# Two local reorderings in a fused attention and feed-forward kernel: the products of the last two row blocks, and one transpose moved from the sync queue to TensorE

**The chip, the cores and the metric.** The kernel runs on one core of one Trainium2 chip. The metric is the device time of one execution in microseconds; the profiled span (first to last instruction) is some 1.8 us shorter than that time in most executions. A run is called fast unless it is over 1.5% above the fastest of its kernel; only fast runs are compared.

## The reference, cut to what matters

Attention with random features for 8 batches of 576 rows, followed by a gated feed-forward layer over all 4608 rows:

```python
q_p, k_p = (phi(q_s), phi(k_s))            # phi: project on omega, exp of (h - max)
kv  = np.einsum('bhsm,bhsd->bhmd', k_p, v)
z   = np.sum(k_p, axis=2)
num = np.einsum('bhsm,bhmd->bhsd', q_p, kv)
den = np.einsum('bhsm,bhm->bhs', q_p, z)[..., None] + 1e-06
x   = (num / den)                           # -> (4608, 512)
g, val = x @ w_gate, x @ w_val
out = (gelu(g) * val) @ w_out
```

## The kernel before

The order of work on each engine is written out by hand, so an engine runs its instructions in program order. The rows are worked off in nine token tiles of 512, while a batch has 576 rows, so a block of 128 x rows can straddle two tiles. A block is normalised by VectorE (`nx`), then transposed into `xT`, either by the sync queue (`xd`) or by TensorE into PSUM and a copy (`xt`, `xc`):

```python
def xd(self, i):
    n, x_sb = self.xs[i]
    put_x(self.b * S + 2 * i * SP, n, lambda dst, o, m: nc.sync.dma_start_transpose(
        out=dst, in_=x_sb[o:o + m, :]))     # put_x: one call for each tile that is touched

def xt(self, i):
    n, x_sb = self.xs[i]
    self.xps[i] = mo_tile([P, N_DM, P], BF16, "xt_ps")      # one of four banks
    for c in range(N_DM):
        nc.tensor.transpose(self.xps[i][:, c, :n], x_sb[:n, c * P:(c + 1) * P], ident[:n, :n])

def xc(self, i, copy):
    put_x(self.b * S + 2 * i * SP, self.xs[i][0],
          lambda dst, o, m: copy(dst, self.xps[i][:, :, o:o + m]))
```

The two matrix products of a row block are done by a scheme of seven half-size products. `pm(s, n, ...)` is product n of row block s; 1, 6, 7 and 4 accumulate in the same bank, out_one, one after the other, and in between the bank is read out: `pa(s, 2)` adds product 7's sum to the right half, `pc` copies product 4's sum as the left half. `pst` stores through two queues, 64 rows each.

```python
        p.pm(0, 7, 0, HF)
        p.pa(0, 2)
        p.pm(0, 4, 0, HF)
        p.pc(0, dve)
        p.pst(0, 1, None, (nc.sync, nc.scalar))
        p.pm(1, 7, 0, HF)
        p.pa(1, 2)
        p.pst(1, 1, 1, (nc.sync, nc.scalar))      # right half
        p.pm(1, 4, 0, HF)
        p.pc(1, dve)
        p.pst(1, 1, 0, (nc.sync, nc.scalar))      # left half
```

In this text "nd group" stands for the eight small products that give one block of num and den, "gate product" for the products with w_gate (g_ps), "kz product" for the 72 that sum k_p with v, "features" for the products with omega (pq, pk) and their exponentials, and "fillers" for products of zeros that nobody reads (fill_ps). A bank is one accumulator of TensorE's output memory; four of them are handed out in turn by `mo_tile`.

The softmax here doesn't subtract the row's maximum and nothing guards it: scores larger than these inputs give would overflow.

## Time and profile before

| | before |
|---|---|
| time, median of 4 runs | 343.07 us (342.66 to 343.44) |
| TensorE busy | 327.4 of 341.0 us |
| TensorE's wait for block 3 of batch 1 | 1.03 us at 66 us |
| its two waits for VectorE in the tail | 0.52 us each |
| last copy to the end of the span | 3.3 us (337.65 to 341.0) |

(41 of TensorE's 3155 matmul records are missing from this profile.) TensorE is all but full, so a microsecond that is saved must come out of one of its waits, or of the closing part after its last product. The profile lines are in the prediction, each with what is to be seen in it.

### The profile page before, as it was taken

The numbers are of one execution on the slowest core, as the hardware profiler recorded it, in microseconds if no ns is written. First come the engines' busy times: TensorE is split into PE (matmuls) and PEld (weight loads), VectorE is DVE, ScalarE is ACT, GpSimd is POOL, SyncE is SP. The second block draws the span as 40 slices with busy tenths as digits, with TensorE's granted clock in tenths as the row PEclk, the third lists the DMA queues.
The fourth block names the chain that finished last, engine by engine and source line by source line (L and its number), as shares of the span: only waits on it lengthen the run. The fifth ranks groups of instructions, "written<-read, shape, count | busy, mean of one in ns | idle before, by whom it ended". The sixth has DMA issues, their size and how long they took to land.

```text
span 341.0 us, 7993 instructions
## 1 busy us (share of the span) xinstructions
PE 327.4 (96%) x3114; PEld 206.0 (60%) x3155; DVE 229.1 (67%) x481; ACT 214.3 (63%) x434; POOL 149.9 (44%) x152
## 2 busy tenths in 40 slices
PE   7889999889999999999999999999999999999994
PEld 3565455566646664566447654665466786686683
DVE  3875388979773768375936683677457777796783
ACT  4894366774778558756875677658765447626640
POOL 8326004033486447744674559477968400000000
PEclk9999999999999999999999999999999999999999
DMA  8999999599889256945498629671413040013004
GB/s 155 275 206 207 206 272 206 137 174 236 178 135 331 49 102 91 326 89 108 60 326 113 116 32 291 164 111 19 94 33 63 8 115 11 1 32 93 2 0 124
DMA packets 67173, 45.08 MB, mean 132 GB/s; under 512 B 47296, under 2 KB 60096, under 8 KB 67136
## 3 DMA queue, kind: packets, MB, share of 16 engines
q0 software_dynamic: 14848, 22.12, 31.4%
q1 hardware_dynamic: 51744, 21.64, 30.4%
q10 hardware_dynamic: 544, 0.82, 0.8%
q8 instruction: 24, 0.39, 0.5%
q14 instruction: 13, 0.11, 0.1%
HBM read 37.78 MB, written 9.44 MB: 138 GB/s over the span
## 4 chain that ended last, share of the span: by engine, by line
PE 83%; DVE 6%; DMA 3%; ACT 3%; issue 2%; POOL 2%; DVEq 0%; POOLq 0%
PE g_ps L433 20%; PE o_ps L559 18%; PE val_one L378 11%; PE val_two L378 9%; PE out_one L533 5%; PE out_two L533 3%; PE v_ps L462 3%; PE g_ps L425 3%; PE kz_ps L285 3%; DMA q_in<-in_q_dram 2%; PE nd L302 2%; PE pk L220 2%; DVE x_sb L314 2%; PE pq L242 2%; DVE val_c L387 1%
## 5 line engine op out<-in xcount | busy, mean ns | idle before, releaser
L433 PE MATMUL g_ps<-xT,w_gate_sb 128*128 128x512 bf16 x352 | 108.2, 379 | 0.5
L440 ACT ACTIVATE g_gelu<-g_ps 128x512 bf16<-128x512 f32 x108 | 63.6, 598 | 54.1 <-PE g_ps L433 25.3
L559 PE MATMUL o_ps<-w_out_sb,gated 128*128 128x512 bf16 x275 | 64.6, 380 | 1.1 <-issue 0.6
L480 POOL TENSOR_TENSOR gated<-g_gelu,val_c 128x512 bf16<-128x512 bf16 x29 | 33.7, 1164 | 52.2 <-DVE iden L313 26.3
L387 DVE TENSOR_TENSOR val_c<-val_one,val_c 128x256 f32<-128x256 f32 x48 | 20.3, 424 | 49.0 <-ACT g_gelu L440 40.0
L378 PEld LDWEIGHTS <-w_val_sb 128*128 128x128 bf16 x384 | 36.5, 98 | 17.3 <-issue 1.4
L559 PEld LDWEIGHTS <-gated 128*128 128x128 bf16 x288 | 26.5, 98 | 33.5 <-issue 3.9
L383 ACT COPY val_c<-val_one 128x256 f32<-128x256 f32 x95 | 35.2, 371 | 11.2 <-PE val_one L378 8.1
L378 PEld LDWEIGHTS <-val_sums 128*128 128x128 bf16 x288 | 27.3, 98 | 24.4 <-DVE x_sb L314 3.7
L249 ACT ACTIVATE q_pT<-pq 128x512 bf16<-128x512 f32 (+1 forms) x68 | 34.6, 598 | 11.7 <-PE pq L242 11.5
L233 DVE TENSOR_REDUCE nmax<-pk 128x8 f32<-128x1024 f32 (+2 forms) x43 | 39.7, 968 | 2.9 <-PE pk L220 1.4
L433 PEld LDWEIGHTS <-w_gate_sb 128*128 128x128 bf16 x376 | 34.9, 98 | 11.2
L228 ACT ACTIVATE k_p<-pk 128x1024 bf16<-128x1024 f32 (+2 forms) x43 | 33.0, 832 | 8.1 <-PE pk L220 6.4
L378 PE MATMUL val_one<-x_sums,w_val_sb 128*128 128x256 bf16 x192 | 36.6, 272 | 0.6 <-DVE val_c L387 0.4
L387 DVE TENSOR_TENSOR val_c<-val_two,val_c 128x256 f32<-128x256 f32 x96 | 36.0, 414 | 0.8 <-PE val_two L378 0.7
L271 POOL TENSOR_TENSOR v_ext<-vf,wk 128x1152 bf16<-128x1152 f32 x12 | 28.2, 2347 | 13.9 <-ACT wk L260 13.9
L484 POOL TENSOR_TENSOR gated<-g_gelu,val_c 128x256 bf16<-128x256 bf16 x34 | 24.1, 711 | 15.0 <-ACT g_gelu L440 15.0
L314 DVE TENSOR_TENSOR x_sb<-nd,iden 128x512 bf16<-128x512 f32 (+2 forms) x41 | 27.8, 677 | 1.4
L564 DVE COPY o_sb<-o_ps 128x512 f32<-128x512 f32 x20 | 13.7, 685 | 19.4 <-PE o_ps L559 14.9
L383 ACT COPY val_c<-val_two 128x256 f32<-128x256 f32 x45 | 16.8, 373 | 11.7 <-PE val_two L378 11.7
L484 DVE TENSOR_TENSOR gated<-g_gelu,val_one 128x256 bf16<-128x256 bf16 x48 | 20.0, 416 | 6.0 <-ACT g_gelu L440 5.7
L378 PE MATMUL val_two<-x_sums,val_sums 128*128 128x256 bf16 x96 | 18.4, 274 | 1.0 <-POOL x_sums L455 0.3
(104 smaller groups left out, 486.3 us busy)
## 6 DMA issues: line engine op xcount, KB each, us to landing
out_dram<-o_sb SPq DMA_DIRECT2D x67, 128.0 KB, 3.3
vf<-in_v_dram POOLq DMA_DIRECT2D x7, 1152.0 KB, 12.4
q_in<-in_q_dram POOLq DMA_DIRECT2D x8, 576.0 KB, 9.4
k_in<-in_k_dram POOLq DMA_DIRECT2D x7, 576.0 KB, 6.2
w_gate_sb<-in_moe_w_gate_dram POOLq DMA_DIRECT2D x3, 512.0 KB, 17.7
w_val_sb<-in_moe_w_val_dram POOLq DMA_DIRECT2D x3, 512.0 KB, 19.4
w_out_sb<-in_moe_w_out_dram POOLq DMA_DIRECT2D x3, 512.0 KB, 13.4
vf<-in_v_dram SPq DMA_DIRECT2D x1, 1152.0 KB, 5.7
```

What stands on the lines that cost most here:

```text
L228: last["begun"] = nc.scalar.activation(self.k_p[:, gs, i0:i0 + n, :], pk, func=Exp)
L233: nc.vector.reduce_max(self.nmax[:, gs, i0:i0 + n], pk, axis=AX, negate=True)
L249: last["begun"] = nc.scalar.activation(dst[:, a, i0:i0 + n], self.pq[c][a].rearrange("m (i e p) -> m i e p", e=2, p=SP), func=Exp)
L314: nc.vector.tensor_mul(x_sb[:n].rearrange("p (g h d) -> p g h d", g=2, h=4)[:, gs], ndv[:, :, :, :D], iden[:n, gs].broadcast_to((n, gs.sto ...
L378: nc.tensor.matmul(ps, w[:, c, self.i * P:(self.i + 1) * P], x[:, c], start=first and c == 0, stop=c == 1, skip_group_check=not first)
L383: copy(self.c[:, {1: 0, 6: 1, 5: 2}[n]], self.beta if n == 5 else self.one)
L387: nc.vector.tensor_add(part, (self.gamma, self.beta, self.one)[k], part)
L433: last["begun"] = nc.tensor.matmul(self.gps[jf], w_gate_sb[:, jm, jf * P:(jf + 1) * P], x_tiles[self.t][:, jm], start=(jm == 0), stop=(jm ...
L440: nc.scalar.activation(self.gelus[jf][:, part], src, func=Gelu)
L480: eng.tensor_mul(self.gated[:, i, :], self.gelus[i], self.v[i].row())
L484: eng.tensor_mul(self.gated[:, i + HF, ts], self.gelus[i + HF][:, ts], s.c[:, 2] if half else s.one)
L559: nc.tensor.matmul(self.ps[qq], self.g.gated[:, f, qq * P:(qq + 1) * P], w_out_sb[:, f, :], start=(jf == 0), stop=(jf == N_DFF - 1))
```

## The change

The intent is to close the two kinds of wait named in the table. In the tail both seventh products go first, so that VectorE reads one block's bank while TensorE works on the other's. Block 3 of batch 1 leaves the queue in which it stood fourth, and goes over TensorE.

```diff
         n.nx(3)
-        n.xd(3)
         m.kf(2, False)
         m.km(2)
         fill(12)
+        n.xt(3)
+        n.xc(3, dve)
         m.kf(3, True)
@@
         p.pm(0, 7, 0, HF)
         p.pa(0, 2)
+        p.pm(1, 7, 0, HF)
+        p.pa(1, 2)
         p.pm(0, 4, 0, HF)
         p.pc(0, dve)
         p.pst(0, 1, None, (nc.sync, nc.scalar))
-        p.pm(1, 7, 0, HF)
-        p.pa(1, 2)
-        p.pst(1, 1, 1, (nc.sync, nc.scalar))
         p.pm(1, 4, 0, HF)
         p.pc(1, dve)
-        p.pst(1, 1, 0, (nc.sync, nc.scalar))
+        p.pst(1, 1, None, (nc.sync, nc.scalar))
```

## The prediction

> **What bounds the kernel now.** I read the page first: its header, the busy line and the chain that ended last.
>
> ```profile
> span 341.0 us, 7993 instructions
> PE 327.4 (96%) x3114; PEld 206.0 (60%) x3155; DVE 229.1 (67%) x481; ACT 214.3 (63%) x434; POOL 149.9 (44%) x152
> ...
> PE 83%; DVE 6%; DMA 3%; ACT 3%; issue 2%; POOL 2%; DVEq 0%; POOLq 0%
> ```
>
> TensorE is busy for 327.4 of 341.0 us, so all of its idle time is 13.6 us, and 83% of the chain is its own work. A change that only reorders work can win no more than the particular holes that it closes. The two parts of this change aim at two different holes, so I then read the chain in order of time around the first one (the columns are start in us, length in us, what):
>
> ```profile
> 62.95 0.42 DVE x_sb L314
> ...
> 63.38 0.76 DVE nmax L233
> ...
> 65.05 2.33 DMA xT<-x_sb
> ...
> 67.57 1.38 POOL x_sums L455
> ```
>
> Between 65.05 and 67.38 the end of the program hangs on a transposing transfer into xT, and then on the Pool subtraction that reads it. The timeline of the same place says what TensorE does meanwhile (start, length, engine, line, operation, and in brackets the idle time before it with its releaser):
>
> ```profile
> 65.95 0.44 PE L302 MATMUL nd<-kz,q_pT 128*64 128x65 bf16 x8
> 67.42 0.61 PE L425 MATMUL g_ps<-xT,w_gate_sb 128*128 128x256 bf16 x4 [1.03 <-DMA xT<-x_sb]
> ```
>
> It stands for 1.03 us. Cutting the sync queue's own timeline into short windows gives the five transposes of batch 1 that are queued there: they are issued at 60.64, 62.43, 63.73, 65.05 and 66.34. The first three are x blocks 0 to 2; the last two are block 3, in two because its 128 rows straddle two token tiles. They land 2.8, 2.4, 2.5, 2.3 and 2.4 us after issue. Block 3 was ready on VectorE at 63.37 (62.95 + 0.42) but its turn in the queue came only at 65.05, and it landed at about 67.4. That is the wait.
>
> The second hole is the tail. The timeline there, TensorE first and then VectorE:
>
> ```profile
> 333.06 0.82 PE L533 MATMUL out_one<-w_out_sb,gated 128*128 128x256 bf16 x6
> 334.40 0.81 PE L533 MATMUL out_one<-out_sums,gated 128*128 128x256 bf16 x6 [0.52 <-DVE o_sb L544]
> 335.05 0.82 PE L533 MATMUL out_one<-w_out_sb,gated 128*128 128x256 bf16 x6
> 336.38 0.81 PE L533 MATMUL out_one<-out_sums,gated 128*128 128x256 bf16 x6 [0.52 <-DVE o_sb L544]
> ```
>
> ```profile
> 333.92 0.42 DVE L544 TENSOR_TENSOR o_sb<-out_one,o_sb 128x256 f32<-128x256 f32 x1 [0.16 <-PE out_one L533]
> 335.25 0.42 DVE L547 COPY o_sb<-out_one 128x256 f32<-128x256 f32 x1 [0.91 <-PE out_one L533]
> 335.90 0.42 DVE L544 TENSOR_TENSOR o_sb<-out_one,o_sb 128x256 f32<-128x256 f32 x1 [0.23 <-PE out_one L533]
> 337.23 0.42 DVE L547 COPY o_sb<-out_one 128x256 f32<-128x256 f32 x1 [0.91 <-PE out_one L533]
> ```
>
> Each row block's fourth product adds onto the bank that its seventh product has just filled, so TensorE waits twice, 0.52 us each, for VectorE to read the seventh one out. After the last copy (337.65) nothing is left but the last stores.
>
> **What the Trainium skill says.** "VectorE: DVE Perf Modes", section "The three transpose paths", gives 390 ns for a 128x128 bf16 transpose on TensorE and 1309 ns by DMA. The trace agrees in kind: one transpose record on TensorE has a median of 218 ns and the records overlap (four start within 0.22 us in the chain), against 2.3 to 2.8 us to landing here. "TensorE: Matmul & The Clock Gate", section "Part 4: PE-mode transpose", adds that the result goes to PSUM and has to be copied out; the trace has the price of such a copy:
>
> ```profile
> L330 PE MATMUL xt_ps<-ident,x_sb x20: 190/218/229, 21.5 to 42.3; 128*128 128x128 bf16 x16, 64*128 64x64 bf16 x4
> ...
> L335 DVE COPY xT<-xt_ps x4: 284/418/425, 22.8 to 42.9; 128x512 bf16<-128x512 bf16 x3, 128x256 bf16<-128x256 bf16 x1
> ```
>
> "DMA: Bandwidth & Descriptors", section "Issuing engines are not separate DMA queues", says that stores issued from two engines run on the same 16 DMA engines and interleave. The trace agrees: of two stores of 128 KB issued together at 333.79, behind an earlier pair, the sync one lands after 2.4 us and the scalar one only after 3.1, where the lone last pair of 64 KB takes 1.9 and 2.2. This matters for the tail.
>
> **Part two, the transpose (first in time).** Removed: two DMA transposes out of the sync queue. Added on TensorE: four transposes, 0.22 us of issue, placed after the fillers and before the next features, where TensorE already waits until about 63.44 for VectorE's block 3. Added on VectorE: two copies of 128x256 (block 3 goes to two tiles) at 0.284 us, about 0.5 us together, between two of the maxima. Their own path: block 3 ready 63.37, transposed by about 63.85; VectorE is in a maximum of 1.22 us from 63.29, so the copies run from 64.42 to about 64.95. Block 3 is thus there 2.4 us earlier than its transfer landed.
>
> What then comes last? Tile 1 also needs block 2, whose transfer is issued at 63.73 and lands at 66.2. And the standing order of TensorE puts the fifth nd group first: 65.95 before, about 0.2 later now, since the transposes push the features, these push the scalar exponentials, and these free its bank. With its 0.26 us of issue (eight at 0.03) that is 66.45. So the gate product that stood until 67.42 starts at about 66.45: **0.97 us** earlier. The Pool subtraction moves from 67.54 to about 66.35.
>
> How much survives? Step by step: the q features at 67.97 need VectorE's delayed maximum and ScalarE's last k exponentials, about 66.9; they move to about 67.1, 0.87 earlier. ScalarE's exponentials of these were at 68.39; its copy of o_ps is now delayed 0.3 to 0.4 by the later wk and ends at about 67.5, so they start there: 0.9 earlier. The next product of that bank was at 69.79 behind ScalarE's copy at 69.36, so also 0.9 earlier. VectorE, 0.5 us loaded at 65, has slack again by the subtraction at 68.97, which was waiting 1.04 us for Pool and moves by about 1.1. Both roads give about 0.9 at the kz product at 73.12. From there to 92 TensorE is busy for 18.69 of 18.88 us (table of windows), and in the later steps hardly anything but TensorE is on the chain, so the shift should arrive at the end whole: I take **0.9 us**, between 0.6 and 1.1.
>
> **Part one, the tail.** Nothing is added; two 64 KB stores of the second block's right half and two of its left half become two of 128 KB. Six matmuls take 0.655 us of issue (334.40 to 335.05), the last ends 0.82 after the first starts. New order: seventh of block 0 at 333.06; seventh of block 1 at 333.71, ends 334.53; VectorE's addition of block 0 unchanged, 333.92 to 334.34; fourth of block 0 at 334.40 as before, with the hole filled; addition of block 1 from 334.56 to 334.98; fourth of block 1 at 335.05, no wait, ends 335.87; copy of block 0 at 335.25 as before, copy of block 1 from 335.90 to 336.32. Compute thus ends 337.65 - 336.32 = 1.33 us earlier.
>
> But the end is a landing, not a copy. Before: last pair issued 337.69, landing 2.2 later, 339.9, and 1.1 us of closing to 341.0. Now 256 KB are issued at 335.70 and 256 KB at about 336.37, 0.67 apart. The same pattern is in the trace: 256 KB at 333.13 and 256 KB at 333.79, where the last one landed 3.1 us after its issue. So the end is 336.37 + 3.1 = 339.5 instead of 339.9: about 0.4 us. If the larger stores landed like a lone pair of 128 KB (2.7) it would be 0.8. I take **0.5 us**, since two thirds of what is won in compute is given back to the transfer of bytes that formerly left earlier.
>
> **Sum.** 343.06 - 0.9 - 0.5 = 341.66; I say 341.6, for the span some 339.6.
>
> **Rivals.** (a) The wait is only replaced at 66: if block 2's landing or the bank behind ScalarE gives no more than half of the hole, part two is worth 0.4 and the time 342.2. For it: both come within 0.3 us of my new start. Against: neither is above 66.5. (b) PSUM rotation: the extra bank for the transposes shifts which bank each later tile takes in the pool of four, one of which is held by an unfinished o_ps and one by the first gate tile. If the gate tile or the q features get a bank that is freed late, TensorE waits as long as before, the 0.5 us on VectorE is a loss, and the time is 342.6 to 343.2. The trace speaks against a large one, as the copies end before 64.99, when the first gate product starts anyway. (c) The gain of part two is swallowed by something timed independently, the loads of the third batch, or by VectorE, up to 92: then only the tail remains, 342.5. Against: these loads are issued behind the very Pool subtraction that moves forward. (d) The tail gives its full 1.3 us because the last stores overlap better: 340.8.
>
> **Range and chances.** My centre is the sum; (a) to (c) bound it above at 342.6, (d) with a full first part below at 340.7. Three runs of before differ by 0.42 us, which is part of the width. Two per cent is 6.9 us, far beyond both holes together (1.03 + 1.33 us), so within 2% is nearly certain; what is left is for a lost overlap that I cannot see.
>
> **What would show it.** Right: the wait of 1.03 us before the second gate product gone or below 0.2, that product at 66.3 to 66.7; three transposes instead of five in the sync queue; the kz product near 72.2; the later steps unchanged in length (35.4 us from one to the next); in the tail the 0.52 us waits gone, the last copy 1.3 us nearer to its first product, and about 2.9 to 3.1 us from last issue to landing. Wrong: a new wait of TensorE on a bank at 64 to 68, ScalarE or VectorE ahead of kz, or a shift at 73 that is gone at 92.

## The result, and the profile after

The changed kernel took 341.95 us (median of 4, 341.57 to 342.13) against 343.07 in the same rounds. A ratio in this text is the mean time of one kernel's fast runs over that of the other's of the same rounds, so it is not quite the ratio of the medians; here it is 0.9966, 95% interval 0.9949 to 0.9983. The means are 341.90 and 343.06, 1.16 us apart. The prediction's 341.6 lies 0.35 below the median, which lies inside the range.

The page of the changed kernel, the same three lines as in the prediction:

```profile
span 340.1 us, 7996 instructions
PE 328.1 (96%) x3118; PEld 206.9 (61%) x3159; DVE 229.5 (67%) x483; ACT 214.3 (63%) x434; POOL 149.5 (44%) x152
...
PE 84%; DVE 7%; issue 2%; ACT 2%; DMA 2%; POOL 1%; SPq 0%; DVEq 0%
```

TensorE has four instructions more, and the transfers' share of the chain went from 3 to 2%. The timeline of TensorE where the first wait was (start, length, engine, line, operation):

```profile
65.73 0.60 PE L425 MATMUL g_ps<-xT,w_gate_sb 128*128 128x256 bf16 x4 [0.27 <-DMA xT<-x_sb]
...
66.69 0.44 PE L302 MATMUL nd<-kz,q_pT 128*64 128x65 bf16 x8
67.06 0.61 PE L425 MATMUL g_ps<-xT,w_gate_sb 128*128 128x256 bf16 x4
```

The second gate product now follows the fifth nd group without a wait in brackets. A wait for a transfer is left at the first gate product, 0.27 us here and 0.17 before; it comes back under "Why the prediction was right". VectorE's two new copies, and the sync queue with three transposes in place of five:

```profile
64.85 0.48 DVE L335 COPY xT<-xt_ps 128x256 bf16<-128x256 bf16 x2
```

```profile
61.06 4.59 SPq L322 DMA_TRANSPOSE xT<-x_sb  x3
```

In this first profile everything up to 60 us ran about 0.4 us later than in that of before, although both kernels have the same instructions there. So positions are best measured from the first nd group of batch 1 (59.23 before, 59.65 after): the second gate product starts 8.19 us after it before and 7.41 after, the kz product 13.89 and 12.93.

The tail, TensorE and then VectorE:

```profile
332.60 1.47 PE L533 MATMUL out_one<-w_out_sb,gated 128*128 128x256 bf16 x12
...
333.94 1.47 PE L533 MATMUL out_one<-out_sums,gated 128*128 128x256 bf16 x12
```

```profile
333.46 0.42 DVE L544 TENSOR_TENSOR o_sb<-out_one,o_sb 128x256 f32<-128x256 f32 x1 [0.16 <-PE out_one L533]
334.11 0.42 DVE L544 TENSOR_TENSOR o_sb<-out_one,o_sb 128x256 f32<-128x256 f32 x1 [0.23 <-PE out_one L533]
334.79 0.42 DVE L547 COPY o_sb<-out_one 128x256 f32<-128x256 f32 x1 [0.25 <-PE out_one L533]
335.45 0.42 DVE L547 COPY o_sb<-out_one 128x256 f32<-128x256 f32 x1 [0.23 <-PE out_one L533]
```

Two runs of twelve matmuls have replaced four of six, and both 0.52 us waits are gone. The last copy ends 3.27 us after the start of the first seventh product (335.87 less 332.60) instead of 4.59: 1.32 us won. But the span ends 4.27 us after that copy instead of 3.31 (read from the trace to the nanosecond, as the span on the page is rounded): 0.96 us of it are given back. The list of transfers shows where. The scalar queue's last store before the change, then after it (engine and operation, count, size, us from issue to landing):

```profile
out_dram<-o_sb ACTq DMA_DIRECT2D x1, 64.0 KB, 2.2
```

```profile
out_dram<-o_sb ACTq DMA_DIRECT2D x1, 128.0 KB, 3.1
```

It is issued at 337.69 before and 335.90 after, so it lands at 339.9 and 339.0; the remaining 1.1 us to the end of the span are the same in both.

### The profile page after: what moved, and what is told of

Its sections match the earlier page's. It is cut to its first block, busy times and chain, and to the rows that moved or that the text cites. A ratio compares the mean times of both kernels' runs of the same rounds, so it can differ in the third digit from the quotient of the medians.

```text
span 340.1 us, 7996 instructions
## 1 busy us (share of the span) xinstructions
PE 328.1 (96%) x3118; PEld 206.9 (61%) x3159; DVE 229.5 (67%) x483; ACT 214.3 (63%) x434; POOL 149.5 (44%) x152
## 4 chain that ended last, share of the span: by engine, by line
PE 84%; DVE 7%; issue 2%; ACT 2%; DMA 2%; POOL 1%; SPq 0%; DVEq 0%
PE g_ps L433 20%; PE o_ps L559 18%; PE val_one L378 11%; PE val_two L378 9%; PE out_one L533 5%; PE out_two L533 3%; PE g_ps L425 3%; PE v_ps L462 3%; PE kz_ps L285 3%; PE pk L220 2%; PE nd L302 2%; DVE nmax L233 2%; PE pq L242 2%; DVE x_sb L314 2%; DVE val_c L387 1%
## 5 line engine op out<-in xcount | busy, mean ns | idle before, releaser
L302 PEld LDWEIGHTS <-q_pT 128*128 128x128 bf16 (+1 forms) x320 | 14.5, 100 | 7.9 <-issue 3.6
```

## The experiments

Twelve runs, four at a time on one chip, five rounds each. The fourth column is the difference of the means of the fast runs, in us, against before in the same rounds; each has an uncertainty of about 0.45 us (the 95% interval of a ratio is some 0.0013 to either side; 0.6 us in the last two rows). The last column is the same difference taken from the spans of the cores: in before the time is 1.73 to 1.86 us longer than the span in every run, but in 14 runs of the other kernels in this table 2.0 to 2.9 us longer, so the two differ by up to 0.3 us. All gave correct results. The medians of "tail only" and of the last row count a slow execution; of the fast ones alone they are 342.56 and 342.84.

| run | median | before | difference | ratio | of spans |
|---|---|---|---|---|---|
| before again | 343.52 | 343.11 | +0.19 | 1.0004 | +0.19 |
| changed, again | 341.63 | 343.11 | -1.50 | 0.9955 | -1.65 |
| tail only | 342.68 | 343.11 | -0.62 | 0.9980 | -0.59 |
| transpose only | 342.19 | 343.11 | -0.92 | 0.9971 | -0.95 |
| changed, one half split off | 341.77 | 343.01 | -1.17 | 0.9965 | -1.40 |
| changed, both halves split off | 341.77 | 343.01 | -1.56 | 0.9955 | -1.75 |
| tail, plus the transpose's cost alone | 342.45 | 343.01 | -0.56 | 0.9984 | -0.75 |
| changed, block 2 too | 343.41 | 343.01 | +0.29 | 1.0009 | -0.04 |
| changed, third time | 341.64 | 343.49 | -1.80 | 0.9948 | -1.80 |
| tail only, again | 342.70 | 343.49 | -0.76 | 0.9978 | -0.76 |
| changed, split with fewer issues | 349.44 | 343.49 | +5.79 | 1.0172 | +5.56 |
| changed, block 2 too, other order | 342.91 | 343.49 | -0.73 | 0.9979 | -1.02 |

And what their profiles give when measured between fixed points: from the first nd group of batch 1 to the kz product of batch 2; from the same group to the k features of the next tile, at about 91 us; from there to the first seventh product of the tail; from that to the end of the last copy; and from that copy to the end of the span.

| profile | first nd group | to kz | to 91 us | 91 to tail | tail to last copy | copy to end |
|---|---|---|---|---|---|---|
| before | 59.23 | 13.89 | 32.35 | 241.48 | 4.59 | 3.31 |
| before again | 59.32 | 14.16 | 32.62 | 241.47 | 4.59 | 3.30 |
| tail only, again | 59.88 | 14.01 | 32.47 | 241.50 | 3.26 | 4.03 |
| tail, plus cost alone | 59.29 | 14.24 | 32.70 | 241.19 | 3.26 | 4.07 |
| changed | 59.65 | 12.93 | 31.39 | 241.56 | 3.27 | 4.27 |
| changed, again | 59.41 | 12.69 | 31.15 | 241.52 | 3.26 | 4.23 |
| changed, third time | 59.78 | 13.12 | 31.58 | 241.56 | 3.27 | 4.25 |
| transpose only | 59.74 | 12.86 | 31.32 | 241.53 | 4.59 | 3.28 |

### Both kernels once more

No edit. For before:

> The kernel before, unchanged, as a control. It should time within 0.2 us of the other runs of before. Open question: in the profiled execution of the changed kernel everything up to 60 us ran 0.42 us later than in that of before (ten fillers at 5.2 us took 1.25 instead of 0.73), where both kernels have the same instructions. If that is chance, a second profile of before will show the fillers at either length and its features for batch 1 (the nd groups) shifted by up to 0.5 us against the first profile; if it belongs to the changed kernel, this profile repeats 0.73 and 59.23 for the first nd group.

and for the changed kernel:

> The changed kernel, unchanged. Theory (predicted sum 0.9 + 0.5): 1.3 to 1.4 us below before. The first measurement gave 1.12. If the late start up to 60 us is chance, a second profile has it smaller, and the distance from the first nd group to the kz product stays 0.9 to 1.0 below that of before (13.89 us there). If it belongs to the change, the gain stays at 1.1 or below and the fillers take 1.25 again.

The fillers took 0.73 us in both new profiles, so the 1.25 is not a property of the changed kernel. It came back in the third profile, though, and in both, the trace's record of the full granted clock begins only at 6.67 and 7.17 us, against 4.83 (before) and 5.12 (changed, again). It does not explain the late start either: "tail only, again" has 0.73 and the latest first nd group of all. The first nd group lies anywhere from 59.23 to 59.88 in these eight profiles, in kernels that are the same up to there: chance of up to 0.65 us, as large as the tail's part of the change. The first measurement gave 1.16 us and the next two 1.50 and 1.80; this is within their intervals, and what made the difference is not shown (the one with 1.80 has the latest start of the three profiles). The third was expected at 1.2 to 1.6, a miss. The three means together (weights 4, 5, 6) are 1.53 us. The control of before against before, +0.19, shows what is noise.

In the second profile of the changed kernel, what TensorE waits for next is plain:

```profile
67.03 0.46 PE L242 MATMUL pq<-qT,omegaT 64*128 64x512 bf16 x2
67.73 0.38 PE L378 MATMUL val_one<-xT,w_val_sb 128*128 128x256 bf16 x2 [0.24 <-ACT o_sb L564]
```

The bank of the first val product is freed by ScalarE's copy of o_ps, which the prediction had reckoned to end at about 67.5.

### Each part alone

Tail only (the second hunk of the diff alone), two runs:

> Only the reordered last two row blocks. My theory: 0.4 to 0.5 us below before, since the last copy ends 1.32 us earlier but the last pair of stores, 128 KB now, lands 3.1 us after issue instead of 2.2. Rival: the compute counts in full and this alone gives 1.2 to 1.3 us (so that the transpose gives nothing or loses).

> Only the reordered row blocks once more, since the profile of the first try fell in an odd run at a quarter of TensorE's speed. 0.4 to 0.7 us below before; in the profile the last copy 1.32 us nearer to the start of block 0's seventh product, the closing part after it 4.1 to 4.3 us instead of 3.3. It also is the proper baseline of the run with the added cost alone, which by an oversight carried the new tail as well (it came 0.55 us below before; if the added cost is hidden, this one comes out within 0.3 us of that).

They gave 0.62 and 0.76 us. The profile of the first was of no use: that one execution took 1182.69 us, while the other four took 342.18 to 342.83. Its products of w_out (duration in ns, least, median, most):

```profile
L559 PE MATMUL o_ps<-w_out_sb,gated x288: 751/1161/1161, 138.4 to 842.6; 128*128 128x512 bf16 x144
```

The normal median is 379 ns. (The "quarter" of the second expectation is rough: the span is 3.5 times the usual one.) It is a slow state of TensorE and not a property of the kernel, so it is left out. The second profile shows 1.33 us won before the last copy (4.59 to 3.26) and some 0.7 given back after it (4.03, just under the 4.1 expected, against 3.30 and 3.31). The rival, 1.2 us and more from the tail alone, is just outside both intervals (0.9966 at the lowest, which is 1.17 us).

Transpose only (the first hunk alone):

> Only block 3 transposed on TensorE. My theory: 0.8 to 1.0 us below before, kz product 0.9 to 1.0 us nearer to the first nd group, the shift still there at 91 us and at the end. Rival: the half microsecond on VectorE and the other waits eat it, 0 to 0.4 us.

It gave 0.92 us, and its kz product is 12.86 us after the first nd group, 1.0 to 1.3 nearer than in the two profiles of before. The rival, 0 to 0.4, falls. On this chip the two parts alone add up to 0.62 + 0.92 = 1.54 us, and both together gave 1.50. The column "91 to tail" says that the shift arrives at the end: the way from there to the tail takes 241.5 to 241.6 us with it and 241.5 without it. (The 241.2 of the next run is taken up in the last section.)

### The cost of the transpose without its gain

The two transfers of block 3 stay; the four transposes and two copies are added, into a tile that nobody reads.

```diff
         n.nx(3)
+        n.xd(3)
         m.kf(2, False)
@@
         n.xt(3)
-        n.xc(3, dve)
+        idle_x = work.tile([P, N_DM, P], BF16, name="idle_x", bufs=1)
+        for o in (0, 64):
+            dve(idle_x[:, :, o:o + 64], n.xps[3][:, :, o:o + 64])
```

> The kernel before, with the four transposes and the two copies of block 3 added, into a scratch tile that nobody reads, while block 3 still goes by the two transfers. This is the cost without the gain. My theory: the extra 0.5 us on VectorE lie under the wait for the transfer, so the second gate product stays where it was (8.2 to 8.5 us after the first nd group) and the time is 0 to 0.3 us above before. Rival: the added work delays the chain by its full 0.5 us or more, and a bank is waited for.

By an oversight it was built on the changed kernel, so it has the new tail too, and "tail only" is its yardstick, not before. It came 0.56 us below before, tail only 0.62 and 0.76 on two other chips: the added work costs between 0.06 and 0.20 us, which is inside the noise (by the spans it costs nothing: 0.75 against 0.59 and 0.76). Its timeline of TensorE:

```profile
66.36 0.44 PE L302 MATMUL nd<-kz,q_pT 128*64 128x65 bf16 x8
67.83 0.61 PE L425 MATMUL g_ps<-xT,w_gate_sb 128*128 128x256 bf16 x4 [1.03 <-DMA xT<-x_sb]
```

The wait is back: 1.03 us, where the three profiles without the added work (before twice, tail only) have 1.03, 0.99 and 0.78; the gate product comes 8.54 us after the first nd group, just over the 8.2 to 8.5 expected. So it belongs to block 3's transfers. That their place in the queue made it, and not their own length, is argued from the times of before: ready at 63.37, turn at 65.05, landing at 67.38, of which a turn at 63.4 would have saved 1.7 us, more than the wait. No run moved the transfer up in the queue. From the second gate product to kz it is 5.69 us here and 5.70 in those three, so the half microsecond on VectorE lies under the wait. A bank that is freed up to 1 us late would be hidden there too, so the rotation is judged from the changed kernel's own profiles, below. One caution: this run also lacks a stop of 0.25 us that those kernels have at 297.6 us (last section), so its time alone cannot exclude a cost of that size.

### Is block 2, the next in the queue, worth the same?

Blocks 2 and 3 both go over TensorE, into one bank, block 2 copied by ScalarE:

```diff
-        n.xd(2)
@@
+        pair = mo_tile([P, 2, N_DM, P], BF16, "xt_ps")      # 8 transposes into it
+        n.xc(2, act)
         n.xc(3, dve)
```

> The changed kernel, with block 2 of batch 1 transposed on TensorE as well (eight transposes into one bank, block 2 copied by ScalarE). In the changed kernel block 2's transfer is the last thing that tile 1 waits for. My theory: nothing much is left to win there, as the second gate product is behind the fifth nd group, which a bank holds back until about 66.1: 0 to 0.3 us below the changed kernel, though the Pool subtraction starts up to 1 us earlier. Rival: the landing of block 2 binds, and it gains 0.4 us or more. A loss would mean that ScalarE, with 0.6 us more before the k exponentials, holds the chain.

It lost all of the gain, +0.29 us against before. The timelines of ScalarE and of TensorE say why:

```profile
64.47 0.58 ACT L335 COPY xT<-xt_ps 128x512 bf16<-128x512 bf16 x1 [2.40 <-PE xt_ps L857]
64.95 1.09 ACT L249 ACTIVATE q_pT<-pq 128x512 bf16<-128x512 f32 x2
```

```profile
66.10 0.29 PE L220 MATMUL pkq<-omegaT,kT 64*128 64x128 bf16 x4 [1.33 <-ACT q_pT L249]
```

ScalarE is in order, and I had put the copy ahead of exponentials whose input TensorE had finished at about 62.9. They waited some 2 us behind it, and TensorE 1.33 us for the bank that they hold. That is an error of placement and says nothing of block 2, so the copy was moved behind those exponentials:

> Block 2 on TensorE as well, now with ScalarE's copy behind the exponentials of the third q chunk instead of ahead of them (in the first try the copy waited for the transposes in ScalarE's order, held those exponentials back by 2.4 us, and TensorE stood 1.33 us for their bank). Theory: no such wait, second gate product 6.9 to 7.3 us after the first nd group, time within 0.3 us of the changed kernel. Rival: block 2's landing was binding, and it gains 0.4 us or more.

This came 0.73 us below before, where the changed kernel of the same rounds came 1.80 below. So it is not the gain that the rival expected, but a loss of about 1.1 us (0.8 by the spans) against the changed kernel, outside my own expectation too. Its profile fell into a slow execution as well (862.39 us, the other five 341.80 to 343.24), so what it waits for is not shown, and stays open.

### The tail: can the stores be had earlier?

The right half of the last block is finished 1.3 us before its left half. First it is stored at once, as before the change:

```diff
         p.pa(1, 2)
+        p.pst(1, 1, 1, (nc.sync, nc.scalar))
@@
-        p.pst(1, 1, None, (nc.sync, nc.scalar))
+        p.pst(1, 1, 0, (nc.sync, nc.scalar))
```

> The changed kernel, with the right half of the last row block stored as soon as its addition is done, as before the change, so that the last pair of stores is 64 KB each again. My theory (the tail is bound by the landing of the last bytes, 3.1 us for the scalar queue's 128 KB behind another pair): the last landing comes 2.4 to 2.6 us after its issue instead of 3.1, from the last copy's end to the end of the span 3.6 to 3.8 us instead of 4.2, the time 0.4 to 0.7 us below the changed kernel. Rival: the closing part after the last copy is a fixed cost or set by the queue's bytes in all, no difference.

This theory fell. The last pair is 64 KB, and still landed 2.8 us (sync) and 3.1 us (scalar) after issue; from the last copy to the end it was 4.33 us, not 3.6 to 3.8, and the gain of 1.17 us is no better than that of the changed kernel (which was not run on this chip). The landing is thus not a matter of the last pair's size alone. In this profile 256 KB are issued at 334.91, only 0.8 and 0.9 us ahead of the last pair, where before the change the last pair came 1.3 us behind another pair of 64 KB; that it queues behind them is the likely reason, but only argued. There is an untested rival: a store makes 80 packets whether it has 64 or 128 KB (five stores a queue make 400, four make 320), so halving it saves bytes but no packets.

Then block 0's right half is split off too:

```diff
         p.pa(0, 2)
+        p.pst(0, 1, 1, (nc.sync, nc.scalar))
@@
-        p.pst(0, 1, None, (nc.sync, nc.scalar))
+        p.pst(0, 1, 0, (nc.sync, nc.scalar))
```

> As the one before, and the right half of the first of the two row blocks is stored early too: four steps of two 64 KB stores about 0.65 us apart. My theory: last landing 2.1 to 2.4 us after issue, 3.3 to 3.5 us from the last copy to the end, the time 0.6 to 0.9 us below the changed kernel. Against it: an issue occupies its queue for 0.5 to 0.7 us, so four of them 0.65 us apart may fall behind, and then it is no better than with one split.

Now the last stores do land fast, but the scalar queue is late with them. Its timeline, and the list of transfers at that time:

```profile
336.14 0.47 ACTq L491 DMA_DIRECT2D out_dram<-o_sb  x1
```

```profile
out_dram<-o_sb SPq DMA_DIRECT2D x1, 64.0 KB, 2.2
out_dram<-o_sb ACTq DMA_DIRECT2D x1, 64.0 KB, 1.9
```

The last copy had ended at 335.30, so the store stood 0.84 us behind the queue's earlier issues, 0.6 to 0.7 us each. It is 3.80 us from copy to end instead of 4.2, but the time, 1.56 us below before, cannot be told from the 1.50 and 1.80 of the changed kernel.

Last, the two right halves as one transfer each, on one queue, to have the queues free:

```diff
+        def one(s, part, queue):
+            ...
+            queue.dma_start(out=out[b * S:(b + 1) * S, ns]
+                            .rearrange("(p r) m -> r p m", r=R)[r:r + 2], in_=p.hi[s][:, ns])
@@
         p.pa(0, 2)
+        one(0, 1, nc.sync)
         p.pm(1, 7, 0, HF)
         p.pa(1, 2)
+        one(1, 1, nc.scalar)
@@
-        p.pst(0, 1, None, (nc.sync, nc.scalar))
+        one(0, 0, nc.sync)
@@
-        p.pst(1, 1, None, (nc.sync, nc.scalar))
+        p.pst(1, 1, 0, (nc.sync, nc.scalar))
```

> Both right halves stored early, each as one transfer of 128 KB on one queue, so that no queue is still issuing when the last pair (64 KB each) is ready. In the run with both halves split the scalar queue issued its last store only 0.84 us after the last copy, since an issue under load takes it 0.6 to 0.7 us. Theory: with the queues free, the last issue comes 0.05 us after the last copy and lands 2.0 to 2.4 us later; 3.3 to 3.6 us from the last copy to the end instead of 4.2; 0.6 to 0.9 us below the changed kernel. Rival: the bytes in flight hold the landing whatever the queues do: 3.8 us or more, 0 to 0.4 us.

It is 5.79 us slower than before, and up to the last copy as fast as the changed kernel; the landings of its last pair make the difference (11.4 us from copy to end):

```profile
out_dram<-o_sb ACTq DMA_DIRECT2D x1, 64.0 KB, 9.1
out_dram<-o_sb SPq DMA_DIRECT2D x1, 64.0 KB, 10.0
```

For some 4 us the DMA engines moved about 49 GB/s with a mean busy share of a tenth, that is some two of sixteen. The Trainium skill has a reason that fits in "DMA: Bandwidth & Descriptors", section "Why a DMA increments its semaphore by 16 and not by 1": the number of engines is the largest, up to 16, that divides the slowest dimension of both access patterns. Here that dimension is 2 on the output's side, where the two transfers of `pst` each begin with 64 rows. The busy share agrees with two engines; the share of each single engine was not read. So this run says nothing about the queues, and no version was found that is clearly better than the changed kernel.

## Why the prediction was right

- **The wait at 66 us.** It was predicted to go, with the second gate product 7.22 us after the first nd group (66.45 less 59.23). It went, and that product came 7.41, 7.08 and 7.57 us after it in the three profiles of the changed kernel. What sets it now is TensorE's own order: it comes 1.33 to 1.35 us after the first gate product, with no wait between. The first gate product in turn waited 0.27 us (first profile) and 0.42 (third) for the queue's second transfer, block 1's, and for no transfer in the second profile, where kz is earliest. The same wait was 0.17 to 0.51 in the profiles without the change. So the gap that is left at this place is block 1's, which the prediction did not look at. Block 3's copies were predicted from 5.19 us after that group on and began at 5.20 in the first profile.
- **Rival (a), that block 2's landing takes over.** It comes close, as was said: the Pool subtraction that needs the whole tile began 7.44, 7.04 and 7.62 us after the group, against 7.12 predicted, since block 2's landing varies. It did not eat the gain.
- **Rival (b), the banks.** Fell: in the changed kernel's profiles the only wait for a bank between 64 and 68 us is the 0.24 us for ScalarE's copy shown above, in the second profile. The copy ends 8.27 to 8.28 us after the first nd group in all three, and the predicted 67.5 is 8.27 after it.
- **The shift reaches kz and the end whole.** Predicted 0.9 us. The transpose alone gave 0.92, and changed less tail only of the same rounds 1.80 - 0.76 = 1.04. From the first nd group to 91 us the mean of the three profiles without the gain (before twice, tail only) is 32.48 and of the four with it 31.36: 1.12 us. So rival (c) fell, and the term was a little small: it was worked out from one profile of before that happens to have the shortest way to kz of the three, 13.89 us against 14.16 and 14.01.
- **The tail.** Every start that the profile shows came true within 0.01 us, counted from the first seventh product: no wait, 1.32 us won at the last copy, the scalar queue's last store landing 3.1 us after issue as in the pair at 333.79. From the seventh product to the end the three profiles of the changed kernel are 0.4 us shorter than before and tail only is 0.6; the timed gain is 0.62 and 0.76. The two figures given were 0.4 and 0.8, and the 0.5 chosen is inside the noise of all of these. Rival (d), the full 1.3 us, fell.
- **The sum.** 1.4 us predicted; 1.16, 1.50 and 1.80 measured, 1.53 over all of them. With 0.5 us to either side of each measurement, this close a match of the sum is in part luck.
- **Slips that cost nothing.** The 13.6 us of TensorE's idle time count the missing records as idle: the complete profile of before has 11.4. The fifth transfer was issued at 66.30, not 66.34.

What was taken from it too lightly was the remedy: that the landing takes 3.1 us was right, but not that a smaller last store would cure it, as the first split run showed.

## What to carry to other kernels

When the profile names a transfer as the releaser, look at its place in the queue: its data may have been ready long before its turn (1.7 us here), and then another way can be worth it, as long as the work put in its place lies under a wait that is still there. When a tail is shortened, follow it to the landing of the last bytes: compute that ends earlier makes the last stores bunch up, and here a half to nearly three quarters of what was won went back to them. Two changes of under 2 us each need several runs and fixed points inside the profile, as the start of the kernel alone varies by half a microsecond.

## What the Trainium skill lacked or had wrong

- "VectorE: DVE Perf Modes", section "The three transpose paths", gives one figure for a transpose by DMA, 1309 ns. In these profiles one 128x512 block took 2.4 to 4.1 us from issue to landing, and two blocks of one execution differed by up to 1.6 us; the issue alone held the sync queue for 1.2 to 2.2 us. The section has nothing on waiting in the queue, which was 1.7 of the 4.0 us from ready to landing here.
- "DMA: Bandwidth & Descriptors", section "Issuing engines are not separate DMA queues", says that issuing from several engines only saves the initiating time, usually small, and gives no figure. At the tail an issue took a queue 0.5 to 0.7 us and the scalar queue fell 0.84 us behind.
- "TensorE: Matmul & The Clock Gate", section "Seeing it yourself", mentions a clock gate seen stuck at a quarter for 50 us and more. Two of the runs here may be like it for a whole execution: in the 1182.69 us run the median product of w_out took 1161 ns instead of 379, in the 862.39 us run 785, and both profiles gave the granted clock as 1.0 all the while. Whether it is the same thing is not shown.
- No page that I found gives a length for a short stop of TensorE's instruction stream in which it waits for nothing that the profile shows. The nearest, "Runtime: NRT & Kernel Launch", section "Instruction fetch mechanics", has a stall of the fetch after a taken branch only, without a length; whether the stops here are of the fetch is not shown. A weight load stood as in the first line below in before, and as in the second in the changed kernel, each worth about 0.25 us when the weight loads of two profiles are lined up. The stops go with the kernel and not with the execution: the first is in every fast profile of before, of tail only and of block 2 too, the second in all seven with block 3's transpose in place (the changed kernel, transpose only, the splits), and the run with the cost alone has neither, which is why its "91 to tail" is 241.2. In the changed kernel they all but cancel against before. So four transposes and two copies more can move such a stop, here a matter of a quarter of a microsecond, nearly half of the tail's gain. The cause is open.

```profile
297.58 0.10 PEld L378 LDWEIGHTS <-w_val_sb 128*128 128x128 bf16 x1 [0.37 <-issue]
```

```profile
112.52 0.28 PEld L302 LDWEIGHTS <-q_pT 128*128 128x128 bf16 x7 [0.24 <-issue]
```
